# Agent attention and a maxout layer on one core: a new order of the whole program, with a rebuilt head, paired value products, five relu slots and split PSUM reads

## The chip, the cores and the metric

One core of a Trainium2 chip runs the whole program. The metric is the time of one execution in microseconds on the device; the kernel before took 438.34 us (median of three runs, 438.05 to 439.25).

## The reference

```
B, N, C, n_agents = 4, 12544, 128, 49;  d_ff = 768
sm(a, b)  = softmax(a @ b.T / sqrt(C))                 # over the last axis
agent_v   = sm(agents, k) @ v                          # 49 x 128 per batch
attn      = sm(q, agents) @ agent_v                    # 12544 x 128 per batch
x         = attn.reshape(50176, 128)
h         = max(max(x @ w1, x @ w2), x @ w3)           # 50176 x 768
out       = h @ w_out                                  # 50176 x 128
```

## The kernel before, in words

The attention output is never formed. For each batch the agents' values (49 x 128, normalised) are multiplied with weight differences into a matrix G: w3-w1 (768 columns at C31), w2-w1 (768 columns at C21), and w1 @ w_out (128 columns at C1O). A query's exponentials over the 49 agents, times G, then give the hidden layer's differences, and max(w1, w2, w3) becomes w1 + max(relu(w3-w1), w2-w1), of which the w1 part goes straight to the output (`li`). The division by the softmax's sum is done at the very end (`ov`).

**Key and value part.** Each batch has 98 tiles of 128 rows of k and v, taken in chunks (`FIRST` for batch 0, `LATER` for the others). For a chunk g of batch b: loads `kl`, `vl` on SP's DMA queue, casts to bf16 `kc`, `vc` (POOL; in batch 0 the values are cast by ACT), a transpose of the keys (batch 0: TensorE `kt` and DVE `ke`; later batches: a DMA transpose `kt` from the buffer KB to KT on SP's queue), scores `ks` (49 columns a tile), exponentials `kx` on ACT, products with the values `kv` on PE, and their addition `va` into VA on DVE. When a batch is done, `nr` normalises, and `gp`/`gv` make and copy G.

**Query part.** 49 steps s of eight tiles (1024 rows). Load `ql`, cast `qc` (POOL), transpose: `qd`, by DMA (QB to QT), for the steps in `TURNED`, else TensorE `qt` and DVE `qe`; scores `sc`, exponentials `ex` on ACT, sums `su`. Then for each of six 128-column blocks f of the hidden layer: `u` (PE, difference w3-w1, 128 x 1024 into a pair of PSUM banks), `a` (ACT relu into a slot of AS), `v` (PE, w2-w1, another pair of banks), `x` (DVE: maximum of v in PSUM and a, into R). Block FI = 4 does it without DVE: ACT relus into PSUM, PE adds, ACT relus into R. The output products `p` go either as full 128-row blocks or as pairs of 64-row blocks (`ROWS`, f or r); `ov` (DVE) scales into OS, `st` stores.

**What sets the order.** Nothing is decided at run time. `ORDER` is a written list of all operations with their slot numbers (`name/slots`); each engine issues its own in that order, and a wait is put wherever an operation needs another's result or slot. SP's one queue carries all loads, the DMA transposes and nearly all stores, and SP issues them in order: a transfer that must wait holds up those behind it. `SLOTS` gives the buffers: 8 PSUM banks (PS), 13 load buffers (LD), 10 output buffers (OS), 4 of KT, 4 of QT, 3 of AS, 13 of R. `SPLIT` marks the blocks whose u lies in two separate banks, which ACT reads as two relus of 512 columns.

**Head.** Before the first u, batch 0 must be through: 12.85 MB of keys and values at one DMA queue, then the weights, in halves. Meanwhile PE runs idle products of the identity (`wm`, `wn`).

Of the kernel before, what the change touches and what calls it, by code (L numbers as in the profile page):

```python
# [9 lines left out]
FP32 = mybir.dt.float32  # L10
BF16 = mybir.dt.bfloat16
# [6 lines left out]
DFF = NF * P  # L18
SCALE = 1.0 / math.sqrt(C)
C31, C21, C1O, WC = 0, DFF, 2 * DFF, 2 * DFF + C  # L20
CV, CT = KT * A, (KT - 1) * A
FI = 4
SPARE = 8
FIRST = [KT] * 10 + [4, 4]
LATER = [KT] * 10 + [8]
TURNED = (10, 13, 15, 18, 22, 24, 25, 28, 29, 30, 31, 32, 33, 34, 35, 36, 37, 38, 39, 40, 41, 42, 43, 44, 45, 46, 47, 48,)
ROWS = """
rrfrff rrrffr ffrfff ffrfrr rfffff rrrrrr ffffff ffffrr fffrff rfrrfr fffffr ffrfrf rrfrrr fffffr fffffr frffrf fffrrr rfffff
ffffff rrrfff ffffrf rrrfff rrffrr ffrrrr rrrrrr ffffff ffffff rrfffr ffrfrr rrrrrr ffffff ffffff fffffr rffrfr rrrrrr ffrffr
rfrrfr frrfff rrfrfr ffrffr rfffrr rrrrrr frffrf rfrfff rfrfff rrrfrr ffrfff rrrrrr rffrff  # L30
""".split()
# [11 lines left out]
ROW, FULL, COL = range(3)  # L43


SLOTS = {"PS": 8, "LD": 13, "QB": 3, "KB": 3, "VB": 4, "KT": 4, "QT": 4, "EQ": 4, "EK": 4, "AS": 3,
# [8 lines left out]
class Plan:  # L55
# [9 lines left out]
    def add(self, name, eng, fn, cost, mode=FULL, after=(), new=(), use=(), serve=0.0, dma=False, sides=None):  # L65
        self.index[name] = len(self.ops)
        for cls, t, *banks in new:
            self.tile(cls, t, *banks)
        self.ops.append(dict(name=name, eng=eng, fn=fn, pace=cost[0], lat=cost[1], mode=mode, after=list(after),
                             use=[x[1] for x in new] + list(use), serve=serve, dma=dma or eng == SP, sides=sides or {}))  # L70
# [89 lines left out]
    def lane(self, o, place, first):  # L160
        if not o["use"]:
            return "AG"
# [45 lines left out]
def graph(plan, em):  # L208
# [3 lines left out]
    add("id0", POOL, em.clear_ident, (0.3, 0.6))  # L212
    add("id", POOL, em.make_ident, (0.3, 0.6), after=["id0"])
    add("ones", DVE, em.make_ones, (1.0, 1.1), after=["id0"])
    add("agl", ACT, em.load_agents, (0.5, 5.0), dma=True)
    add("agc", DVE, em.cast_agents, (0.42, 0.52), after=["agl"])
    add("agt", PE, em.turn_agents, (0.2, 0.4), after=["agc", "id"], new=[("PS", "agt")])
    add("prep", DVE, em.place_agents, (0.4, 0.5), after=["agt", "ones"], use=["agt"])
    ch = chunks(0)
    for g, (t0, n) in enumerate(ch):  # L220
# [4 lines left out]
        add(f"kt0.{g}", PE, em.k_turn(g, n), mm(n, 128), after=[f"kc0.{g}", "prep"], new=[("PS", f"kT_ps0.{g}", 3)], use=[f"kb0.{g}"])  # L225
# [3 lines left out]
            new=[("EK", f"e0.{g}")], use=[f"s0.{g}"])  # L229
        add(f"to0.{g}", PE, em.totals(g, n), mm(1, n * 49), after=[f"kx0.{g}"], use=[f"e0.{g}", plan.tile("PS", "acc")])  # L230
# [3 lines left out]
        if m < n:  # L234
            add(f"vd0.{g}", DVE, em.cast("v", "vb", 0, t0, n, DVE, m, n), ((n - m) * 0.067 + 0.08, (n - m) * 0.067 + 0.2),
                after=[f"vl0.{g}"], use=[f"v0.{g}", f"vb0.{g}"])
        add(f"kv0.{g}", PE, em.first_values(g, n), mm(n, 49), after=[f"to0.{g}", f"vc0.{g}"] + ([f"vd0.{g}"] if m < n else []),
            use=[f"vb0.{g}", f"e0.{g}", "acc"])
    for g in range(SPARE):
        add(f"wm.{g}", PE, em.warm(f"warm.{g}"), (0.2225, 0.45), after=["id"], new=[("PS", f"warm.{g}")])  # L240
    for g in range(len(ch)):
        add(f"wn.{g}", PE, em.warm(f"warn.{g}", 2), (0.445, 0.67), after=["id", f"vl0.{g}"], new=[("PS", f"warn.{g}")])
    last = len(ch) - 1
    for w in ("w1", "w3", "w2"):
        add(f"l{w}a", SP, em.w_load(w, 0, DFF // 2), new=[("LD", w)], **dma(196))
        add(f"l{w}b", SP, em.w_load(w, DFF // 2, DFF), use=[w], **dma(196))
    add("lwo", SP, em.w_load("wo", 0, DFF), new=[("LD", "wo")], **dma(393))
    add("d31a", DVE, em.differences(C31, "w3", "w1", ((0, DFF // 2),)), (0.43, 0.55), after=["lw1a", "lw3a"], use=["w1", "w3"])
    add("d31b", DVE, em.differences(C31, "w3", "w1", ((DFF // 2, FI * P), (FI * P + P, DFF))), (0.42, 0.54), after=["lw1b", "lw3b"],
        use=["w1", "w3"])  # L250
    add("d32", DVE, em.differences(C31, "w3", "w2", ((FI * P, FI * P + P),)), (0.21, 0.33), after=["lw2b", "lw3b"], use=["w2", "w3"])
    add("d21a", DVE, em.differences(C21, "w2", "w1", ((0, DFF // 2),)), (0.43, 0.55), after=["lw2a", "lw1a"], use=["w1", "w2"])
    add("d21b", DVE, em.differences(C21, "w2", "w1", ((DFF // 2, DFF),)), (0.43, 0.55), after=["lw2b", "lw1b"], use=["w1", "w2"])
    add("cw1", ACT, em.cast_w1, (0.74, 0.87), after=["lw1a", "lw1b"], use=["w1"])
    add("tw1", PE, em.turn_w1, mm(NF, 128), after=["cw1", "prep"], new=[("PS", "tw1")])
    add("ew1", DVE, em.evacuate_w1, dve_half(DFF), after=["tw1"], use=["tw1"])
    add("cwo", POOL, em.cast_wo, (0.77, 0.85), after=["lwo"], use=["wo"])
    add("rs0", DVE, em.reduce_first, (0.5, 0.6), after=[f"to0.{g}" for g in range(last + 1)], new=[("KR", "kr0")], use=["acc"])
    add("rc0", DVE, em.recip_first, (0.35, 0.4), after=["rs0"], use=["kr0"])
    add("nr0", DVE, em.normalise_first, (0.13, 0.25), after=["rc0"] + [f"kv0.{g}" for g in range(last + 1)], new=[("G", "G0")],  # L260
        use=["kr0", "acc"])
    half = DFF // 2
    for name, c, d, eng in (("a", C31, ["d31a"], ACT), ("b", C31 + half, ["d31b", "d32"], DVE), ("c", C21, ["d21a"], ACT),
                            ("d", C21 + half, ["d21b"], DVE)):
        add(f"gp{name}", PE, em.product(0, c, c + half, f"gp{name}"), mm(1, half), mode=COL, after=["nr0"] + d, new=[("PS", f"gp{name}")])
        add(f"gv{name}", eng, em.product_out(0, c, c + half, c, f"gp{name}", eng), act(half) if eng == ACT else dve(half),
            after=[f"gp{name}"], use=[f"gp{name}", "G0"])
    add("pl", PE, em.prep_linear, mm(NF, 128), after=["ew1", "cwo"], new=[("PS", "pl")])
    add("el", ACT, em.evacuate_linear, (0.17, 0.31), after=["pl", "ones"], use=["pl"])
    add("gl", PE, em.product(0, C1O, WC, "gl"), mm(1, C), mode=COL, after=["nr0", "el"], new=[("PS", "gl")])  # L270
    add("gvl", ACT, em.product_out(0, C1O, WC, C1O, "gl", ACT), act(C), after=["gl"], use=["gl", "G0"])


    for b in range(1, B):
        ch = chunks(b)
        for g, (t0, n) in enumerate(ch):
# [11 lines left out]
            add(f"kv{r}", PE, em.values(b, g, n, m), mm(n, 49), after=[f"kx{r}", f"vc{r}"], use=[m, f"vb{r}", f"e{r}"])  # L288
            add(f"va{r}", DVE, em.add_values(b, g, m), (0.13, 0.25), after=[f"kv{r}"] + ([f"va{b}.{g - 1}"] if g else []),
                use=[m, plan.tile("VA", f"va{b}")])  # L290
# [7 lines left out]
        add(f"to{b}", PE, em.total(b, g, n, m), (n * 0.0253 + 0.1, n * 0.0253 + 0.335), after=[f"fo{b}", f"kv{r}"],  # L298
            use=[m, f"es{b}", f"e{r}"])
        held = [f"gp{x}" for x in "abcd"] + ["gl"] if b == 2 else [f"gp{x}{b - 2}" for x in "abcdl"] if b > 2 else []  # L300
        add(f"kr{b}", DVE, em.reciprocal_of(b, m), (0.25, 0.3), after=[f"to{b}"], new=[("KR", f"kr{b}")], use=[m])
        add(f"nr{b}", DVE, em.normalise(b, m), (0.25, 0.32), after=[f"kr{b}", f"va{r}"] + held, new=[("G", f"G{b}")],
            use=[f"kr{b}", f"va{b}"])
        for name, c0, c1, eng in (("a", C31, C31 + half, ACT), ("b", C31 + half, C21, DVE), ("c", C21, C21 + half, ACT),
                                  ("d", C21 + half, C1O, DVE), ("l", C1O, WC, ACT)):
            w = c1 - c0
            add(f"gp{name}{b}", PE, em.product(b, c0, c1, f"gp{name}{b}"), mm(1, w), mode=COL,
                after=[f"nr{b}", "el", "d31a", "d31b", "d32", "d21a", "d21b"], new=[("PS", f"gp{name}{b}")])
            add(f"gv{name}{b}", eng, em.product_out(b, c0, c1, c0, f"gp{name}{b}", eng), act(w) if eng == ACT else dve(w),
                after=[f"gp{name}{b}"], use=[f"gp{name}{b}", f"G{b}"])  # L310
# [744 lines left out]
```

## Time and profile before

| what | value |
|---|---|
| median of three runs | 438.34 us |
| span of the profiled execution | 436.6 us; the page gives no other time of it |
| granted TensorE clock, mean | 0.996 |
| PE / DVE / ACT / POOL busy | 411.9 / 386.6 / 393.9 / 170.0 us |
| first u on PE | 41.41 us |
| moved by DMA | 122.37 MB, mean 280 GB/s |
| DMA transposes | 33 of keys, 28 of queries |

A busy share is the time in which an instruction of the engine is under way. On ACT and DVE the records of neighbours overlap, so what an instruction costs in a row of them is the distance from its start to the next one's. The tile names are the buffer classes above, with `ps` for the PSUM banks. All instructions carry the line of the helper that records them, so that the rows are told apart by tiles and shapes.

### The profile page before, as it was taken

How to read it: one execution, taken by the hardware profiler on the slowest of the kernel's cores; microseconds unless marked ns; L12 is line 12 of the kernel's file. 1: busy time of each engine (PE TensorE's matmuls, PEld its weight loads, DVE VectorE, ACT ScalarE, POOL GpSimd, SP SyncE). 2: the span in 40 equal slices, each digit the busy share in tenths (PEclk: the TensorE clock that was granted, in tenths of full speed). 3: DMA queues.
4: the chain of work that ended last, by engine and by line, in shares of the span. 5: the costliest groups of instructions: out<-in, count | busy, mean ns of one | idle time of the engine just before them, and what ended most of it. 6: DMA issues, size and time to landing. Idle time of an engine off the chain costs nothing.

```text
span 436.6 us, 14853 instructions
## 1 busy us (share of the span) xinstructions
PE 411.9 (94%) x6488; PEld 256.9 (59%) x6488; DVE 386.6 (89%) x470; ACT 393.9 (90%) x486; POOL 170.0 (39%) x177
## 2 busy tenths in 40 slices
PE   1788999999999999999999999999999999999994
PEld 1464565666666566656656655656656555655574
DVE  1435999999999999999998999899999999999994
ACT  1278999999999999999999899999999999999993
POOL 3541565556655535165525445342531111000000
PEclk9989999999999999999999999999999999999999
DMA  8999999999999999999999999996999994266313
GB/s 310 411 410 383 311 334 372 289 281 343 269 318 342 279 371 298 266 339 285 294 345 261 407 247 278 276 326 143 276 363 290 284 306 98 74 208 208 119 71 125
DMA packets 98107, 122.37 MB, mean 280 GB/s; under 512 B 71479, under 2 KB 74235, under 8 KB 98043
## 3 DMA queue, kind: packets, MB, share of 16 engines
q1 hardware_dynamic: 97552, 121.07, 95.2%
q8 instruction: 51, 0.84, 0.8%
q10 hardware_dynamic: 491, 0.36, 0.3%
q14 instruction: 13, 0.11, 0.1%
HBM read 78.74 MB, written 25.69 MB: 239 GB/s over the span
## 4 chain that ended last, share of the span: by engine, by line
PE 69%; ACT 16%; DVE 7%; DMA 4%; issue 2%; POOL 1%; SPq 0%; POOLq 0%
PE ps L388 69%; ACT AS L388 9%; DVE R L388 6%; DMA LD<-in_k_dram 4%; ACT R L388 2%; ACT ps L388 2%; POOL KB L388 1%; DVE OS L388 1%; ACT EQ L388 1%; ACT VB L388 1%; ACT G L388 1%; ACT EK L388 1%; ACT OS L388 0%; SPq L388 0%; DVE QT L388 0%
## 5 line engine op out<-in xcount | busy, mean ns | idle before, releaser
L388 DVE TENSOR_TENSOR R<-ps,AS 128x1024 bf16<-128x1024 f32 x245 | 293.5, 1219 | 15.1 <-PE ps L388 10.7
L388 ACT ACTIVATE AS<-ps 128x1024 bf16<-128x1024 f32 (+1 forms) x259 | 245.8, 987 | 10.0 <-PE ps L388 7.2
L388 PE MATMUL ps<-EQ,G 49*128 49x512 bf16 (+1 forms) x1248 | 203.3, 370 | 3.5 <-ACT AS L388 0.7
L388 PE MATMUL ps<-wo_bf,R 64*128 64x128 bf16 (+1 forms) x3368 | 194.0, 218 | 1.1 <-issue 0.8
L388 PEld LDWEIGHTS ps<-wo_bf,R 64*128 64x128 bf16 (+1 forms) x3368 | 139.5, 95 | 59.4 <-issue 31.3
L388 PEld LDWEIGHTS ps<-EQ,G 49*128 49x128 bf16 x1248 | 56.4, 93 | 63.8 <-DVE R L388 18.3
L388 POOL CAST QB<-LD 128x1024 bf16<-128x1024 f32 x49 | 50.5, 1040 | 94.6 <-DMA QT<-QB 49.8
L388 POOL CAST KB<-LD 128x1152 bf16<-128x1152 f32 (+2 forms) x45 | 49.8, 1115 | 52.1 <-DMA LD<-in_k_dram 41.8
L388 DVE TENSOR_TENSOR OS<-ps,RC 128x512 f32<-128x512 f32 x96 | 65.4, 682 | 2.6 <-PE ps L388 2.2
L388 POOL CAST VB<-LD 128x1152 bf16<-128x1152 f32 (+1 forms) x33 | 37.4, 1136 | 40.7 <-DMA LD<-in_v_dram 36.5
L388 ACT ACTIVATE ps<-ps 128x1024 f32<-128x1024 f32 x49 | 49.9, 1018 | 2.8 <-PE ps L388 2.2
L388 ACT ACTIVATE R<-ps 128x1024 bf16<-128x1024 f32 x49 | 50.3, 1027 | 1.9 <-PE ps L388 1.6
L388 ACT ACTIVATE EK<-ps 128x441 bf16<-128x441 f32 (+2 forms) x45 | 23.4, 535 | 18.8 <-PE ps L388 18.4
L388 POOL TENSOR_TENSOR EA<-EA,EK 128x441 f32<-128x441 f32 x27 | 27.6, 1022 | 25.4 <-ACT EK L388 25.1
L388 ACT ACTIVATE EQ<-ps 128x512 bf16<-128x512 f32 x49 | 29.9, 610 | 1.0 <-PE ps L388 0.5
L388 DVE COPY KT<-ps 128x1152 bf16<-128x1152 bf16 (+1 forms) x12 | 8.2, 701 | 14.0 <-PE ps L388 14.0
L388 PE MATMUL ps<-QT,agT 128*64 128x512 bf16 (+1 forms) x104 | 19.9, 388 | 0.2
L388 PE MATMUL ps<-G,EQ 49*128 49x128 bf16 x392 | 19.1, 217 | 0.0
L388 PE MATMUL ps<-EK,VB 128*128 128x49 bf16 x392 | 17.4, 186 | 1.6 <-ACT VB L388 1.6
L388 PEld LDWEIGHTS ps<-EK,VB 128*128 128x128 bf16 x392 | 13.9, 97 | 8.1 <-ACT EK L388 4.2
L388 PE MATMUL ps<-agT,KT 128*128 128x49 bf16 x392 | 17.4, 186 | 0.4 <-DVE KT L388 0.4
L388 PEld LDWEIGHTS ps<-agT,KT 128*128 128x128 bf16 x392 | 14.4, 98 | 4.7 <-issue 2.1
(59 smaller groups left out, 177.6 us busy)
## 6 DMA issues: line engine op xcount, KB each, us to landing
LD<-in_q_dram SPq DMA_DIRECT2D x48, 512.0 KB, 7.7
out_dram<-OS SPq DMA_DIRECT2D x48, 512.0 KB, 6.2
LD<-in_k_dram SPq DMA_DIRECT2D x40, 576.0 KB, 7.6
LD<-in_v_dram SPq DMA_DIRECT2D x40, 576.0 KB, 8.4
LD<-in_k_dram SPq DMA_DIRECT2D x3, 512.0 KB, 5.3
LD<-in_v_dram SPq DMA_DIRECT2D x3, 512.0 KB, 6.7
LD<-in_moe_w_dram SPq DMA_DIRECT2D x6, 192.0 KB, 10.6
KT<-KB SPq DMA_TRANSPOSE x33, 7.3
```

What stands on the lines that cost most here:

```text
L388: i = call(*args, **named)
```

## The change

- **Head.** Batch 0 comes in twelve chunks of 8 tiles and one of 2 (`FIRST`), all keys ahead of nearly all values. Ten of the value chunks are loaded into the output buffers OS, exponentials of batch 0 go into R slots, and scratch tiles of their own (agents, w1) go into R slots too. The casts of the values are dealt out by `VCAST` (seven to POOL, five to ACT, one to DVE). The weights come in three pieces (128, 256, 384 columns, `CUTS`) instead of two, and the first G is made in matching pieces. The cast of w1 goes to POOL and behind the first step's products, and w_out is loaded behind that.
- **Values in pairs.** For batches 1 to 3 the value products of two chunks go into one bank of their own, followed by one addition: 18 `va` instead of 33. They no longer share the bank of the scores.
- **Splits.** `SPLIT` now knows u (two relus), v (two maxima of 512 columns) and b (both): 85 blocks of 245 have split relus (14 before), 72 split maxima (none before). An operation d, for a DVE relu in block FI, is written and not used.
- **Slots.** AS has five slots instead of three.
- **Linear part.** G's last part is stored twice, each for 64 rows with zeros in the other half (`gz`), so that `li` could also run as full blocks; `LINEAR` uses the old way for all 49.
- **Query turns.** Steps 20, 21 and 23 are turned by DMA too: 31 `qd` instead of 28.
- **64-row blocks.** 116 of 294 output blocks are pairs of 64 rows, 127 before.
- **Order and slots** of the whole program are new.

```
-FIRST = [KT] * 10 + [4, 4]
+CUTS = {"a": (0, P), "b": (P, 3 * P), "c": (3 * P, DFF)}
+FIRST = [GT] * 12 + [2]
-TURNED = (10, 13, 15, 18, 22, 24, 25, 28, ...
+TURNED = (10, 13, 15, 18, 20, 21, 22, 23, 24, 25, 28, ...
 SPLIT = """
-...... u..... .u.... ...... ...... ...... ...... ...... ...... ...... .u.u.. uu.... ...
+vvv..b vbvv.v .u.u.. b..u.u v.uu.v bbbb.u ...u.u .uub.u v.vb.b .uub.. .u.u.u vvuu.v ...
...
+LINEAR = "bbbbbbbbbbbbbbbbbbbbbbbbbbbbbbbbbbbbbbbbbbbbbbbbb"
+VCAST = "pppaappapaapd"
+CASTW = "p"
+OUTS = ("aaaaadd", "addda", "addda", "adada")
-SLOTS = {"PS": 8, "LD": 13, "QB": 3, ... "EK": 4, "AS": 3,
+SLOTS = {"PS": 8, "LD": 13, "QB": 3, ... "EK": 4, "AS": 5,
...
-        add(f"vl0.{g}", SP, em.kv_load("v", 0, t0, n), new=[("LD", f"v0.{g}")], **dma(n * 65.536))
+        add(f"vl0.{g}", SP, em.kv_load("v", 0, t0, n), new=[("OS" if g < 10 else "LD", f"v0.{g}")], **dma(n * 65.536))
...
-        m = n if n == KT else 2
-        add(f"vc0.{g}", ACT, em.cast("v", "vb", 0, t0, n, ACT, 0, m), act(m * 128), after=[f"vl0.{g}"], new=[("VB", f"vb0.{g}")],
+        eng = ENGINES[VCAST[g]]
+        add(f"vc0.{g}", eng, em.cast("v", "vb", 0, t0, n, eng, 0, n), act(n * 128), after=[f"vl0.{g}"], new=[("VB", f"vb0.{g}")],
             use=[f"v0.{g}"])
...
-            add(f"kv{r}", PE, em.values(b, g, n, m), mm(n, 49), after=[f"kx{r}", f"vc{r}"], use=[m, f"vb{r}", f"e{r}"])
-            add(f"va{r}", DVE, em.add_values(b, g, m), (0.13, 0.25), after=[f"kv{r}"] + ([f"va{b}.{g - 1}"] if g else []),
+            if g % 2 or g == len(ch) - 1:
+                two = [(x, ch[x][1]) for x in range(g // 2 * 2, g + 1)]
+                y, h = f"{b}.{g // 2}", f"y{b}.{g // 2}"
+                add(f"kv{y}", PE, em.values(b, two, h), mm(sum(x[1] for x in two), 49), after=[f"{z}{b}.{x}" for x, _ in two for z in ("kx", "vc")],
+                    new=[("PS", h)], use=[f"{z}{b}.{x}" for x, _ in two for z in ("vb", "e")])
+                add(f"va{y}", DVE, em.add_values(b, g // 2, h), (0.13, 0.25), after=[f"kv{y}"] + ([f"va{b}.{g // 2 - 1}"] if g > 1 else []),
...
+                if SPLIT[s][f] in "vb":
+                    vs = [f"{v}.{h}" for h in range(2)]
+                    add(v, PE, em.hidden(vs, s, f, C21, True), pe, mode=ROW, after=[f"ex.{s}"] + needs(1), new=[("PS", x) for x in vs],
+                        use=[e] + gs)
+                    for h in range(2):
+                        add(f"x.{s}.{f}.{h}", DVE, em.max_second(vs[h], s, f, h), (0.6, 0.72), after=[v, f"{a}.{h if SPLIT[s][f] == 'b' else 0}"],
+                            use=[vs[h], a, r])
```

Three places of the order, before and after. In these rows a name is a buffer (its number is the compiler's), `OUT<-IN`, then the shape; `LD` are load buffers, `KB`/`QB` cast keys and queries, `KT`/`QT` their transposes.

First, SP's queue in the second half of batch 3. The row `KT_104<-KB_96 128x9x128` before (row 197 of SP) is the key transpose of that batch's chunk 9, the last of 9 tiles:

```order
L388 DMA_TRANSPOSE QT_105<-QB_93 128x8x128
L388 DMA LD_86<-in_q_dram 128x1024
L388 DMA_TRANSPOSE KT_104<-KB_95 128x9x128
L388 DMA out_dram<-OS_139 128x1024
L388 DMA_TRANSPOSE QT_108<-QB_92 128x8x128
L388 DMA LD_82<-in_v_dram 128x1152
L388 DMA_TRANSPOSE KT_104<-KB_96 128x9x128
L388 DMA LD_86<-in_k_dram 128x1024
```

After, the same transpose is `KT_99<-KB_90 128x9x128`, row 212 of SP:

```order
L416 DMA_TRANSPOSE QT_103<-QB_87 128x8x128
L416 DMA LD_84<-in_q_dram 128x1024
L416 DMA LD_77<-in_v_dram 128x1152
L416 DMA_TRANSPOSE QT_104<-QB_88 128x8x128
L416 DMA LD_78<-in_k_dram 128x1152
L416 DMA out_dram<-OS_144 128x1024
L416 DMA LD_86<-in_q_dram 128x1024
L416 DMA LD_79<-in_v_dram 128x1152
L416 DMA_TRANSPOSE KT_99<-KB_90 128x9x128
L416 DMA_TRANSPOSE KT_100<-KB_92 128x8x128
```

It stood behind 196 transfers and now stands behind 209: the key load of 512 KB that followed it is now far ahead, and so are three more query loads and four more query transposes; the other five are loads of the head in more pieces.

Second, PE around the scores of that chunk (`ps<-agT,KT`), before:

```order
L388 MATMUL ps<-EQ_109,G_149 128x512 x4
L388 MATMUL ps<-wo_bf,R_132 128x128 x4
L388 MATMUL ps<-wo_bf,R_120 128x128 x4
L388 MATMUL ps<-agT,KT_104 128x49 x9
L388 MATMUL ps<-EQ_109,G_149 128x512 x6
```

and after:

```order
L416 MATMUL ps<-EQ_105,G_147 128x512 x4
L416 MATMUL ps<-wo_bf,R_120 128x128 x4
L416 MATMUL ps<-wo_bf,R_124 128x128 x4
L416 MATMUL ps<-agT,KT_99 128x49 x9
L416 MATMUL ps<-EQ_105,G_147 128x512 x6
```

The scores have kept their place among the hidden products (rows 914 and 916 of PE); what has moved is the transpose on SP's queue.

Third, ACT at the end of the head, before (`VB<-LD` casts values, `G` is the first G, `AS` the first relus):

```order
L388 ACTIVATE VB_99<-LD_90 128x1152
L388 ACTIVATE VB_100<-LD_80 128x1152
L388 ACTIVATE EQ_112<-ps 128x512
L388 ACTIVATE VB_97<-LD_82 128x1152
L388 ACTIVATE w_bf<-LD_85 128x768
L388 ACTIVATE G_147<-ps 128x384 x2
L388 ACTIVATE AS_117<-ps 128x1024
```

and after:

```order
L416 ACTIVATE VB_96<-OS_140 128x1024
L416 ACTIVATE VB_94<-OS_143 128x1024
L416 ACTIVATE G_145<-ps 128x256
L416 ACTIVATE G_145<-ps 128x128
L416 ACTIVATE G_145<-ps 128x256
L416 ACTIVATE G_145<-ps 128x128
L416 ACTIVATE AS_113<-ps 128x1024
```

The last value casts have gone to POOL, the cast of w1 too, the query exponentials stand earlier, and four smaller copies of G stand where two larger ones stood.

More of the change, by code (lines that the diff above doesn't have):

```diff
@@ L63, in tile, with add @@
         return name
-    def add(self, name, eng, fn, cost, mode=FULL, after=(), new=(), use=(), serve=0.0, dma=False, sides=None):
+    def add(self, name, eng, fn, cost, mode=FULL, after=(), new=(), use=(), serve=0.0, dma=False, sides=None, lane=None):
         self.index[name] = len(self.ops)
@@ L252, in graph @@
[L252 to L256, printed above, removed]
+    for x, (c0, c1) in CUTS.items():
+        cuts = ((c0, FI * P), (FI * P + P, c1)) if x == "c" else ((c0, c1),)
+        add(f"d31{x}", DVE, em.differences(C31, "w3", "w1", cuts), dve(c1 - c0), after=[f"lw1{x}", f"lw3{x}"], use=["w1", "w3"])
+        add(f"d21{x}", DVE, em.differences(C21, "w2", "w1", ((c0, c1),)), dve(c1 - c0), after=[f"lw1{x}", f"lw2{x}"], use=["w1", "w2"])
@@ new lines, in graph @@
+                add(f"a.{s}.{f}.0", ACT, em.relu(u, u, None), (0.917, 1.076), after=[u], use=[u])
+                add(v, PE, em.hidden([u], s, f, C21, False), pe, mode=ROW, after=[f"a.{s}.{f}.0"] + needs(1), use=[u, e] + gs)
+                if SPLIT[s][f] == "d":
+                    add(f"x.{s}.{f}.0", DVE, em.relu(r, u, None, DVE), (1.14, 1.28), after=[v], use=[u, r])
+                else:
+                    add(f"x.{s}.{f}.0", ACT, em.relu(r, u, None), (0.917, 1.076), after=[v], use=[u, r])
@@ L352, in graph @@
                 else:
-                    add(u, PE, em.hidden([u], s, f, C31, True), pe, mode=ROW, after=[f"ex.{s}"] + needs("a", "b"), new=[("PS", u, 3)], use=[e] + gs)
-                    add(a, ACT, em.relu(a, u, None), (0.917, 1.076), after=[u], use=[u, a])
-                add(v, PE, em.hidden([v], s, f, C21, True), pe, mode=ROW, after=[f"ex.{s}"] + needs("c", "d"), new=[("PS", v, 3)], use=[e] + gs)
-                add(f"x.{s}.{f}", DVE, em.max_second(v, s, f), (1.14, 1.28), after=[v] + ([f"{a}.{h}" for h in range(2)] if two else [a]),
-                    use=[v, a, r])
@@ L358, in graph @@
-        lin = ["gvl" if p[0] == 0 else f"gvl{p[0]}" for p in parts]
+                    add(u, PE, em.hidden([u], s, f, C31, True), pe, mode=ROW, after=[f"ex.{s}"] + needs(0), new=[("PS", u, 3)], use=[e] + gs)
+                    add(f"{a}.0", ACT, em.relu(a, u, None), (0.917, 1.076), after=[u], use=[u, a])
+                if SPLIT[s][f] in "vb":
[5 more added lines that the diff above has]
+                            use=[vs[h], a, r])
+                else:
+                    add(v, PE, em.hidden([v], s, f, C21, True), pe, mode=ROW, after=[f"ex.{s}"] + needs(1), new=[("PS", v, 3)], use=[e] + gs)
+                    add(f"x.{s}.{f}.0", DVE, em.max_second(v, s, f, None), (1.14, 1.28), after=[v] + [f"{a}.{h}" for h in range(1 + (SPLIT[s][f] == "u"))],
+                        use=[v, a, r])
```

651 lines of the change are left out of this document (348 added, 303 removed).

## The prediction

> **What bounds the kernel now.** I read the page first (span, busy shares, the row of the DMA engines), then the busy time by stage, then the waits, then the transfers by kind, and last single stretches of the timeline.
>
> ```profile
> span 436.6 us, 14853 instructions
> PE 411.9 (94%) x6488; PEld 256.9 (59%) x6488; DVE 386.6 (89%) x470; ACT 393.9 (90%) x486; POOL 170.0 (39%) x177
> ...
> DMA  8999999999999999999999999996999994266313
> ```
>
> Three engines stand near 90%, so none of them alone is the answer. The last line is the one that I follow: the DMA engines are full in every slice up to the 34th of 40, and idle behind it. By stage, from the busy time in stretches (the last two numbers of a row are the DMA share and GB/s):
>
> ```profile
> 10.00:20.00 10.00, 7.44 (x87) 5.08 (x86) 4.11 (x7) 2.22 (x6) 5.33 (x6) 1.00 1.03 412
> ...
> 50.00:100.00 50.00, 49.49 (x821) 31.48 (x820) 47.88 (x58) 47.24 (x59) 28.47 (x28) 1.00 1.11 320
> ...
> 300.00:350.00 50.00, 49.44 (x752) 29.57 (x750) 48.27 (x56) 48.78 (x60) 15.86 (x19) 1.00 1.07 283
> 350.00:400.00 50.00, 49.56 (x768) 29.63 (x766) 48.52 (x53) 48.93 (x57) 5.20 (x5) 1.00 0.57 173
> 400.00:425.00 25.00, 24.76 (x442) 15.73 (x442) 24.25 (x26) 23.82 (x28) 0.00 (x0) 1.00 0.33 116
> ```
>
> Between 10 and 20 us nothing but loads is under way, many deep, and the share reads 1.03: that is what a full queue looks like here. From 50 to 350 us it reads 1.07 to 1.11. From 350 us on it falls to 0.57 and 0.33: there the transfers are done and ACT and DVE set the pace, with DVE idle 1.73 + 1.48 + 0.75 = 4.0 us between 300 and 425 us. The waits say the same from the other end:
>
> ```profile
> POOL KB L388 <- DMA LD<-in_k_dram: 41.8, 17, 5.9
> POOL VB L388 <- DMA LD<-in_v_dram: 36.5, 18, 4.6
> ...
> PEld ps L388 <- DVE R L388: 18.6, 74, 0.6
> ...
> PEld ps L388 <- ACT AS L388: 16.0, 61, 0.6
> ```
>
> POOL starts a key or value cast when the load lands, 35 times. PE itself never stands long for a transfer; it waits 0.1 to 0.6 us at a time for a PSUM bank that DVE or ACT still reads. So up to about 330 us two limits run side by side, the bank turnover and the transfer queue, and I have to price the queue.
>
> **The price of a transfer.** Transfers by kind, of the 250 us in which the share is full, and of the loads alone in the head:
>
> ```profile
> q1 hardware_dynamic: 66112, 75.88, 109.2%
> ...
> LD<-in_v_dram SPq DMA_DIRECT2D x29, 576.0 KB, 7.4
> LD<-in_k_dram SPq DMA_DIRECT2D x28, 576.0 KB, 7.6
> LD<-in_q_dram SPq DMA_DIRECT2D x31, 512.0 KB, 8.1
> out_dram<-OS SPq DMA_DIRECT2D x22, 512.0 KB, 6.5
> LD<-in_k_dram SPq DMA_DIRECT2D x2, 512.0 KB, 6.0
> LD<-in_v_dram SPq DMA_DIRECT2D x2, 512.0 KB, 6.9
> KT<-KB SPq DMA_TRANSPOSE x30, 7.5
> QT<-QB SPq DMA_TRANSPOSE x13, 7.3
> ```
> ```profile
> DMA packets 1772, 6.51 MB, mean 407 GB/s; under 512 B 196, under 2 KB 320, under 8 KB 1770
> ```
>
> At 407 GB/s a tile of 128 rows (65.5 KB) takes 0.161 us, a 512 KB transfer 1.29 us. The loads and stores of the 250 us are 57 x 9 + 57 x 8 = 969 tiles, 156 us. If the queue was full, the remaining 94 us went to the 43 transposes, 372 tiles: 0.253 us a tile, 2.0 us for a query tile's transpose of 8. That is the upper end. The lower end is their bytes alone at 407 GB/s: 0.64 us for 256 KB; then 64 of the 250 us would have been idle, which a share of 109% does not allow. The full share is the nearer row, so I take 2.0 us, and treat what the queue lay idle as time that comes back.
>
> **The change, part by part.** *Transfers.* Batch 3's key transpose of chunk 9 is SP's row 197 before and row 212 after, and PE's scores on it stand at nearly the same place (rows 914 and 916). Counted along the queue, 8 more transfers lie ahead of it in the new order: three query loads, one key load of 512 KB (which followed it before) and four query transposes (three because query tiles 20, 21 and 23 are now turned by DMA, one because a later tile's is issued sooner). The other five places are loads cut finer, with the same bytes. Work ahead of it: 4 x 1.29 = 5.2 us, and 4 x 2.0 = 8.1 us, together 13.3 us. What it had to spare:
>
> ```profile
> 292.76 0.49 SPq L388 DMA_DIRECT2D LD<-in_v_dram  x1
> 300.52 1.45 SPq L388 DMA_TRANSPOSE KT<-KB  x1
> ```
> ```profile
> DMA to landing us min/median/max: 3.2/3.8/4.5
> ```
> ```profile
> 298.91 1.14 POOL L388 CAST VB<-LD 128x1152 bf16<-128x1152 f32 x1 [4.62 <-DMA LD<-in_v_dram]
> ...
> 314.48 1.04 POOL L388 CAST VB<-LD 128x1024 bf16<-128x1024 f32 x1 [2.10 <-DMA LD<-in_v_dram]
> ```
> ```profile
> 306.78 0.39 PE L388 MATMUL ps<-agT,KT 128*128 128x49 bf16 x9
> ```
>
> It was issued at 300.52 and landed at the earliest 3.2 us later, 303.7; PE used it at 306.78: 3.1 us to spare. SP issued nothing between 293.3 and 300.5 (it stood before this transpose), and the value load that it had issued last was cast from 298.9, as soon as it had landed, so the queue lay empty for some 3 us. In the new order SP has a backlog there, and those 3 us come back. So PE meets this tile late by 13.3 - 3.1 = 10.2 us at the upper end, and by 7.2 us with the 3 us back; each further microsecond that the queue was idle in the 306 us before takes one off, down to no lateness at all (the first rival). I take **+6 us**, since one gap is seen and the share leaves little room for others. What is late next is everything behind those scores in PE's order (the hidden products of step 32 and 33), and through them ACT and DVE, which run dry; the queries' transposes behind it on SP are late by as much.
>
> The Trainium skill's page "DMA: Bandwidth & Descriptors", section "Latency and other measured facts", gives a DMA transpose an effective 261 GB/s: 1.0 us for a query tile and 1.1 for a key tile, estimates from that page. By it the 43 transposes would fill 47 of the 94 us, the queue would have idled for the other 47 and taken the new transfers without lateness, and the time would be that of the first rival. The share of 109% speaks against it.
>
> *Head.* The last value cast, and what follows it:
>
> ```profile
> 38.47 1.16 ACT L388 ACTIVATE VB<-LD 128x1152 bf16<-128x1152 f32 x1
> 39.66 0.84 ACT L388 ACTIVATE w_bf<-LD 128x768 bf16<-128x768 f32 x1
> ...
> 41.90 3.87 ACT L388 ACTIVATE AS<-ps 128x1024 bf16<-128x1024 f32 x4
> ```
>
> The same bytes must land first, so the landing does not move. The cast goes to POOL, where 1024 columns take 1.04 us (the POOL row at 314.48) against 1.16 here, and no longer stands behind ACT's other casts; the first copies are 256 wide instead of 384. That is -0.7 us (0 to -1.5), and it is spent where PE next waits for a transfer: nothing of it reaches the end.
>
> *Splits, pairs, turns.* Start to start, back to back:
>
> ```profile
> 199.04 1.23 DVE L388 TENSOR_TENSOR R<-ps,AS 128x1024 bf16<-128x1024 f32 x1
> 200.18 0.68 DVE L388 COPY QT<-ps 128x1024 bf16<-128x1024 bf16 x1
> 200.78 0.45 DVE L388 TENSOR_TENSOR VA<-ps,VA 128x49 f32<-128x49 f32 x2
> ...
> 202.61 0.68 DVE L388 TENSOR_TENSOR OS<-ps,RC 128x512 f32<-128x512 f32 x1
> 203.21 1.22 DVE L388 TENSOR_TENSOR R<-ps,AS 128x1024 bf16<-128x1024 f32 x1
> ```
> ```profile
> 202.90 1.02 ACT L388 ACTIVATE AS<-ps 128x1024 bf16<-128x1024 f32 x1
> 203.81 0.59 ACT L388 ACTIVATE EQ<-ps 128x512 bf16<-128x512 f32 x1
> 204.30 1.02 ACT L388 ACTIVATE R<-ps 128x1024 bf16<-128x1024 f32 x1
> ```
>
> DVE's maximum holds it 1.14 us, a PSUM read of half the width 0.60; a split costs 0.06. ACT: 0.91 against 0.49, 0.07. The table goes from 14 to 85 split relus and from none to 72 split maxima: ACT +5.0 us, DVE +4.3. DVE loses 15 value additions of at most 0.22 (-3.3) and three query copies of 0.60 (-1.8): -0.8 in sum. PE loses three query turns. It gets 22 more full-array output blocks, and before such blocks it paid:
>
> ```profile
> L388 PEld LDWEIGHTS ps<-wo_bf,R 128*128 128x128 bf16 x1336 | 75.6, 97 | 34.2 <-issue 28.8 <-DVE OS L388 2.7 <-DVE VA L388 0.7
> ```
>
> 28.8 us over 334 groups of four is 0.09 us each, +1.9 us. None of this moves the end before 306.8 us, where the transfers cover it. What the splits buy is that the first bank of a pair comes free about half a read sooner (0.91 - 0.49 or 1.14 - 0.60), and the pairs of value products no longer hold a scores bank. After the late tile that can win at most DVE's idle time of 4.0 us; I take half, -2.0 (0 to -4.0), and +0.5 for the splits that lie there. The fifth relu slot I cost at nothing: no row of the waits has ACT waiting for a relu slot. POOL's seven value casts in the head (7.3 us) lie beside a POOL that is half idle (5.33 of 10 us); if that cover fails, the last cast is late by one cast, 1.0 us.
>
> Sum: 436.6 + 6.0 - 2.0 + 0.5 = 441.1 us span. The runs' median, 438.34, is 1.74 above the profiled span (the page gives no other time of that execution), so **442.8 us**.
>
> **Rivals.** *Faster: the queue has room after all.* Then 8 more transfers cost nothing, and the head and the banks show. DVE is idle 2.1 us between 50 and 100 us; five such stretches and the later 4.0 make 14.6 us, ACT's extra 5.0 us come off, and I take half of the rest, -4.8. 436.6 - 0.7 - 4.8 + 1.7 = 432.8 us. For it: PE has no long wait for a transfer now, and SP did leave the queue empty at 299. Against it: the share. It decides if the queue idled for about 10 of the 306 us before that tile, which is all that it takes: a mean transpose of 1.95 us instead of 94 / 43 = 2.19. The rule of 261 GB/s lies far on that side of the point.
>
> *Slower for another reason: the engines.* Transfers hidden, no idle time won, ACT's 5.0 us added and the head's 0.7 taken off: 442.6 us. Against it: ACT's waits are for PE's banks, which come free sooner.
>
> *No change:* late by 2 to 3 us at chunk 9, and as much won back behind it: 438 us.
>
> **How the numbers follow.** Late transfers 0.52, engines 0.08, no change 0.13, room in the queue 0.27. Runs of this kernel spread by 0.3%, about 1.3 us, which I take as the bound of "same". So slower 0.60, same 0.13, faster 0.27. The likeliest case by itself reaches from 438 (3 us late, 4.0 us won back) to 449 (10.2 us late, nothing won back: 436.6 + 10.2 + 0.5 + 1.7). Downward the range takes in the slower half of the faster case: 434 to 449.
>
> **What would show it.** In the new profile PE's scores of batch 3, chunk 9, start between 309 and 316 us, after an idle time put down to a transpose; the DMA share stays at 1.07 or more past 340 us; POOL's waits for loads grow; PE has waits of over 1 us that it lacks now. If instead those scores start before 306 us and the share falls below 1.0 earlier, the queue had room and I am wrong on the price of a transpose. The first relu should start near 41.2 us.

## The result and the profile after

The changed kernel takes 443.31 us (median of 14 runs, 439.56 to 446.28); the kernel before, run beside it, 438.67 us (14 runs, 437.89 to 440.07). The ratio is 1.0095, with a 95% interval of 1.0071 to 1.0119. The medians are 4.6 us apart; the ratio, which leaves out one of the 14 executions (446.28 us) because it ran in the chip's slower state, gives 4.2 us. The profiled execution took 444.69 us, with a span of 442.3, so 2.39 us lie outside the span, against 1.74 before; over all runs it is 2.35 against 1.78.

The head of the new page, with the row of the granted TensorE clock:

```profile
span 442.3 us, 14868 instructions
PE 418.7 (95%) x6396; PEld 262.0 (59%) x6396; DVE 388.5 (88%) x529; ACT 389.7 (88%) x553; POOL 178.8 (40%) x190
...
PEclk9999999999999799999989999999999999999998
DMA  8999999999999999999999999999998919346216
```

The clock row before:

```profile
PEclk9989999999999999999999999999999999999999
```

PE is busy 6.8 us longer than before with fewer instructions, and the clock row has a 7 and an 8 where it had 9s. By stage (after the length come PE, its weight loads, DVE, ACT and POOL, busy us with the number of instructions; then the clock, the DMA share and GB/s), first after:

```profile
100.00:150.00 50.00, 47.55 (x687) 29.56 (x686) 46.68 (x64) 46.73 (x72) 26.94 (x29) 0.99 1.09 320
150.00:200.00 50.00, 49.80 (x736) 30.85 (x735) 46.51 (x64) 45.84 (x65) 26.14 (x26) 0.94 1.12 291
200.00:250.00 50.00, 48.32 (x759) 30.04 (x759) 44.05 (x63) 46.42 (x71) 22.46 (x25) 0.97 1.08 309
...
300.00:350.00 50.00, 49.34 (x719) 29.51 (x716) 47.86 (x62) 48.61 (x67) 18.04 (x20) 1.00 1.01 282
350.00:400.00 50.00, 49.65 (x760) 29.54 (x758) 48.95 (x56) 49.03 (x61) 4.26 (x5) 1.00 0.48 137
400.00:425.00 25.00, 24.78 (x387) 14.80 (x388) 24.91 (x30) 24.70 (x33) 0.00 (x0) 1.00 0.40 128
```

and three of these stages before:

```profile
100.00:150.00 50.00, 49.77 (x752) 30.30 (x750) 47.85 (x61) 47.77 (x63) 30.77 (x33) 1.00 1.10 316
150.00:200.00 50.00, 49.82 (x796) 31.51 (x797) 47.85 (x57) 48.36 (x59) 21.97 (x21) 1.00 1.12 302
200.00:250.00 50.00, 49.76 (x821) 31.10 (x819) 46.38 (x58) 47.08 (x62) 25.14 (x27) 1.00 1.10 324
```

The loss lies between 100 and 250 us, not past 306. Matching the first hidden product of each step by the order gives the lateness against before: +0.6 us at step 12 (140.5 us against 139.9), +5.2 at step 13, +3.8 at step 20, +6.5 at step 22 (234.9 against 228.4), and +6.3 still at step 32. The first jump, on POOL and then on PE:

```profile
130.82 1.15 POOL L416 CAST VB<-LD 128x1152 bf16<-128x1152 f32 x1
138.71 1.15 POOL L416 CAST KB<-LD 128x1152 bf16<-128x1152 f32 x1 [6.73 <-DMA LD<-in_k_dram]
145.31 1.15 POOL L416 CAST KB<-LD 128x1152 bf16<-128x1152 f32 x1 [5.45 <-DMA LD<-in_k_dram]
146.40 1.04 POOL L416 CAST QB<-LD 128x1024 bf16<-128x1024 f32 x1
147.39 1.15 POOL L416 CAST KB<-LD 128x1152 bf16<-128x1152 f32 x1
148.48 1.15 POOL L416 CAST VB<-LD 128x1152 bf16<-128x1152 f32 x1
```
```profile
149.69 0.93 PE L416 MATMUL ps<-EK,VB 128*128 128x49 bf16 x18 [2.06 <-POOL VB L416]
```

POOL takes its casts in order and stands 6.73 us for the load of batch 2's key chunk 4 and then 5.45 us for that of chunk 3. Behind both stands the value cast of chunk 1 (148.48), though SP had issued the load of its tile at 91.15 us. PE wants that cast for the pair of chunks 0 and 1 and waits 2.06 us. In the new order ten more transfers lie ahead of chunk 3's key load (three value, two key and two query loads, a store, a key and a query transpose). SP issues it as the second of two at 134.6 us, where it stood at 119.9 before. That these ten transfers make it late is read from the order and these times; no run put the load back. SP's rows of after, then of before:

```profile
91.15 0.33 SPq L416 DMA_DIRECT2D LD<-in_v_dram  x1
...
134.11 0.94 SPq L416 DMA_DIRECT2D LD<-in_k_dram  x2
```
```profile
119.87 0.77 SPq L388 DMA_DIRECT2D LD<-in_k_dram  x1
```

The second jump is the same with chunk 10's value cast, behind a key load that POOL waits 1.73 us for:

```profile
222.99 1.14 POOL L416 CAST KB<-LD 128x1152 bf16<-128x1152 f32 x1 [1.73 <-DMA LD<-in_k_dram]
...
224.40 1.04 POOL L416 CAST VB<-LD 128x1024 bf16<-128x1024 f32 x1
```
```profile
225.58 0.37 PE L416 MATMUL ps<-EK,VB 128*128 128x49 bf16 x8 [1.15 <-ACT R L416]
```

The profile puts this PE wait down to an ACT instruction that ended at about the same time; the product reads POOL's cast, which ends at 225.43. After both of these waits PE runs at half its clock:

```profile
145.00:150.00 5.00, 2.94 (x45) 1.77 (x42) 3.31 (x3) 3.58 (x7) 4.69 (x5) 0.93 1.01 410
150.00:155.00 5.00, 5.00 (x51) 2.82 (x50) 3.94 (x6) 3.02 (x4) 2.21 (x3) 0.50 1.25 182
155.00:160.00 5.00, 5.00 (x102) 3.56 (x98) 3.27 (x4) 4.05 (x8) 0.00 (x0) 0.89 1.11 160
225.00:230.00 5.00, 4.28 (x44) 2.21 (x46) 3.13 (x7) 3.52 (x5) 3.02 (x5) 0.78 1.24 306
230.00:235.00 5.00, 4.82 (x90) 3.15 (x84) 3.81 (x5) 4.32 (x6) 0.00 (x0) 0.88 1.07 228
```

From 150 to 155 us PE is fully busy and does half the matmuls of the next five. The clock that is missing adds up to (0.07 + 0.50 + 0.11) x 5 = 3.4 us at the first place and (0.22 + 0.12) x 5 = 1.7 at the second. A busy PE at 0.50 looks like no idle time at all; only the clock column shows it.

### The profile page after: what moved, and what is told of

It is laid out like the page before. It is cut to its first block, busy times and chain, and to the rows that moved or that the text cites. A ratio compares the mean times of both kernels' runs of the same rounds, so it can differ in the third digit from the quotient of the medians.

```text
span 442.3 us, 14868 instructions
## 1 busy us (share of the span) xinstructions
PE 418.7 (95%) x6396; PEld 262.0 (59%) x6396; DVE 388.5 (88%) x529; ACT 389.7 (88%) x553; POOL 178.8 (40%) x190
## 4 chain that ended last, share of the span: by engine, by line
PE 55%; DMA 11%; ACT 11%; DVE 8%; issue 7%; POOL 6%; SPq 1%; POOLq 0%; DVEq 0%
PE ps L416 55%; ACT AS L416 6%; DVE R L416 6%; DMA LD<-in_k_dram 5%; DMA LD<-in_v_dram 3%; DMA KT<-KB 3%; POOL VB L416 2%; ACT R L416 2%; POOL KB L416 2%; ACT ps L416 1%; POOL QB L416 1%; DVE OS L416 1%; SPq L416 1%; POOL EA L416 1%; ACT EQ L416 1%
## 5 line engine op out<-in xcount | busy, mean ns | idle before, releaser
L416 DVE TENSOR_TENSOR R<-ps,AS 128x512 bf16<-128x512 f32 (+1 forms) x317 | 297.5, 974 | 15.6 <-PE ps L416 10.9
L416 ACT ACTIVATE AS<-ps 128x1024 bf16<-128x1024 f32 (+1 forms) x330 | 250.4, 816 | 12.0 <-PE ps L416 9.6
L416 PE MATMUL ps<-wo_bf,R 64*128 64x128 bf16 (+1 forms) x3286 | 197.1, 219 | 0.6 <-ACT EK L416 0.3
L416 PEld LDWEIGHTS ps<-wo_bf,R 64*128 64x128 bf16 (+1 forms) x3286 | 142.0, 96 | 63.1 <-issue 34.2
L416 ACT ACTIVATE R<-ps 128x1024 bf16<-128x1024 f32 (+1 forms) x58 | 54.7, 946 | 9.2 <-PE ps L416 9.0
L416 POOL CAST VB<-LD 128x1152 bf16<-128x1152 f32 (+1 forms) x34 | 38.4, 1138 | 23.0 <-DMA LD<-in_v_dram 22.3
L416 ACT ACTIVATE EK<-ps 128x441 bf16<-128x441 f32 (+2 forms) x37 | 19.7, 537 | 18.7 <-PE ps L416 18.6
L416 DVE COPY KT<-ps 128x1024 bf16<-128x1024 bf16 (+1 forms) x13 | 8.3, 658 | 10.8 <-PE ps L416 10.8
L416 PEld LDWEIGHTS ps<-G,EQ 49*128 49x128 bf16 x392 | 13.8, 96 | 4.9 <-PE ps L416 0.9
L416 PE MATMUL ps<-EK,VB 128*128 128x49 bf16 x320 | 12.0, 187 | 3.7 <-POOL VB L416 2.6
```

Of the source, the lines that this page charges most:

```text
L416: i = call(*args, **named)
```

## The experiments

Theory A: two waits behind POOL's order and the half clock behind them are the loss. Theory B: the transfers are late, and these places only show it. Theory C: the splits load the engines. The kernel before took 438.81 us beside the first eight kernels (two groups of four), 438.89 beside the next three and 438.41 beside the last.

**The two casts ahead.** Rows of the order table moved:

```diff
- vc2.3 kc2.4 kc2.3 qc.15 kc2.2 vc2.1 qc.16
+ vc2.3 vc2.1 kc2.4 kc2.3 qc.15 kc2.2 qc.16
- vc3.3 ea2.9 fo2.0 kc3.2 fo2.1 vc2.10 fo2.2
+ vc3.3 vc2.10 ea2.9 fo2.0 kc3.2 fo2.1 fo2.2
```

> The changed kernel with two value casts moved ahead in POOL's order: chunk 1 of batch 2 ahead of the two key casts that wait for their loads, chunk 10 of batch 2 ahead of the key cast of batch 3's chunk 2. Theory A (two PE waits behind POOL's order, and the halved TensorE clock after each, are the whole loss): PE's waits of 2.2 us near 148 and 1.2 us near 225 are gone, the granted clock reads 1.00 from 50 to 425 us, and the time falls by 5 to 8 us, to 435.5 to 438.5. Theory B (the full transfer queue sets the pace, these waits are only where it shows): PE waits at the next late transfer instead, the time stays within 1.5 us of 443.3. Theory C (the added splits load the engines): the waits go and the time stays at 442 to 443.

443.99 us (ratio 1.0132, 1.0105 to 1.0159). Theory A fell. Both waits are gone, and the kernel runs ahead of before until step 18 (194.4 us against 195.5); then PE meets other transfers. Busy time by stretch, and the PE timeline of the profile:

```profile
150.00:155.00 5.00, 5.00 (x100) 3.11 (x94) 4.57 (x6) 4.79 (x8) 0.00 (x0) 1.00 1.13 150
195.00:200.00 5.00, 2.73 (x55) 2.09 (x54) 2.88 (x4) 2.80 (x6) 2.54 (x3) 1.00 1.26 244
205.00:210.00 5.00, 2.27 (x24) 1.07 (x22) 3.07 (x5) 3.66 (x4) 2.24 (x2) 1.00 0.84 235
210.00:215.00 5.00, 4.15 (x62) 3.09 (x64) 1.46 (x2) 1.60 (x2) 0.00 (x0) 0.70 1.08 265
```
```profile
210.85 0.41 PE L416 MATMUL ps<-QT,agT 128*64 128x512 bf16 x2 [3.57 <-DMA QT<-QB]
```

The tile that PE waits for here is the transpose of query tile 21, one of the three newly turned by DMA. Ahead of it PE waits 1.10 and 1.16 us for the transposes of key chunks 8 and 7.

**PE kept busy through the two waits.**

```diff
+FILL = {'2.0': 9, '2.5': 5}
+add(f"wf{y}", PE, em.warm(h, FILL[y]), ..., new=[("PS", h)])   # ahead of kv{y} in the order
```

> The changed kernel with 9 and 5 extra 512-column matmuls on PE (0.22 us each, their results overwritten by the products behind them), put just ahead of the two pairs of value products that wait for POOL, so that PE is busy while it would have waited. Theory A, with the clock as a loss of its own: the lateness of the waits stays, the granted clock stays at 1.00 near 150 and 228 us, and the time falls by 3 to 5 us, to 438 to 440.5. If the halved clock costs nothing because DVE and ACT set the pace there, or if it follows from something else than PE's idleness: 443 to 444. Theory B: 443 to 444.

442.92 us (1.0102, 1.0069 to 1.0135). In its profile the clock stays at 1.00, and step 13 starts at 156.9 us instead of 160.9, though 1.6 of these 4.0 us it had already at step 12, ahead of the first wait. PE then waits 1.15 us for query tile 21's transpose, and the median moves by 0.4 us only. Being late by less there means meeting the transfers earlier.

**One cast behind, in the kernel before.**

```diff
- vc2.0 kc2.3 qc.15 (kv2.0 on PE) vc2.1
+ kc2.3 qc.15 vc2.1 vc2.0 (kv2.0 on PE)
```

> The kernel before with one value cast (chunk 0 of batch 2) moved behind the next value cast in POOL's order, which waits for its load until 137.6 us: PE, which wants the product at 136.7, should wait some 3 us (until 139.9). Theory A: the granted clock falls to 0.50 for 3 to 7 us behind the wait, and the time grows by more than the wait, by 4 to 6.5 us, to 442.5 to 445. If a wait costs only itself: +2 to +3, 440.7 to 441.7. If the transfer queue gets ahead during the wait and gives it back: +0 to +1, 438.7 to 439.7.

444.51 us (1.0135, 1.0116 to 1.0155), +5.7. The wait was longer than planned, 4.6 us on PE, since the load landed later. POOL's row, PE's row and the stretches:

```profile
138.80 2.24 POOL L388 CAST VB<-LD 128x1152 bf16<-128x1152 f32 x2 [4.55 <-DMA LD<-in_v_dram]
```
```profile
141.09 0.55 PE L388 MATMUL ps<-EK,VB 128*128 128x49 bf16 x9 [4.57 <-POOL VB L388]
```
```profile
135.00:140.00 5.00, 1.53 (x16) 0.62 (x12) 2.08 (x4) 2.61 (x4) 1.20 (x2) 1.00 1.14 280
140.00:145.00 5.00, 3.91 (x29) 1.88 (x31) 2.15 (x4) 1.89 (x3) 5.00 (x5) 0.55 1.08 400
145.00:150.00 5.00, 5.00 (x72) 2.94 (x68) 3.22 (x4) 3.62 (x5) 1.78 (x3) 0.77 1.14 271
```

**The same with PE kept busy.**

```diff
+add("wf", PE, em.fill(m, 27), mm(27, 384), use=[m])   # ahead of kv2.0 in the order
```

> The kernel of cast_behind (444.5) with 27 matmuls of 384 columns (0.16 us each, 4.4 us, into a part of the bank that nothing reads afterwards) put ahead of the product that waits 4.7 us for its cast, so that PE is busy through the wait. If PE's idleness is what halves its clock, and the halved clock is part of the loss: the granted clock stays at 1.00 from 135 to 150 us and the time falls by 1.5 to 3 us, to 441.5 to 443. If the halved clock costs nothing because DVE and ACT have to catch up anyway: 444 to 445.

441.16 us (1.0052, 1.0033 to 1.0071), a little below what I expected. The late product alone costs 2.3 us; the half clock costs the other 3.35 us (each with some 1.2 us of uncertainty). The clock missing in the rows above is (0.45 + 0.23) x 5 = 3.4 us, so here, by the medians, all of it reached the end.

**Light stores, both kernels.**

```diff
-queue.dma_start(out[r, :]...("(p j) c -> p j c", j=n), os[:, cut, :])
+queue.dma_start(out[r, :]...("(p j) c -> p j c", j=n)[:, :1, :], os[:, cut.start:cut.start + 1, :])
```

> The changed kernel with every store cut to one of its eight 64-column blocks (64 KB instead of 512 KB; the other rows of the output are not written), so that the queue has some 1.1 us less to do for each of the stores. Theory B and theory A agree that the loads then land early enough: no PE wait over 1 us between 50 and 425 us, clock at 1.00, and the gain of the banks shows: 431 to 436. Theory C (engines, splits): the time stays at 440 to 443.

> The kernel before with every store cut to one of its eight 64-column blocks (the other rows of the output are not written), as in light_after, which took 436.9. If the kernel before was held by the queue too, as I argued from its full share: 434 to 436.5, and the change is worth nothing even with room in the queue. If it was held by banks and engines: 438 to 439, and the rest of the change is worth 1.5 to 2 us once the queue has room.

After: 436.86 us (0.9958, 0.9938 to 0.9977), just above my 431 to 436. Before: 437.16 (0.9966, 0.9953 to 0.9979), between my two values. As expected, the profile of light_after has the clock at 1.00 throughout, and PE's longest wait between 50 and 425 us is 0.93 us. The lighter queue gives the changed kernel 443.31 - 436.86 = 6.45 us and the kernel before 438.81 - 437.16 = 1.65. The difference, 4.8 us, is the whole loss: theory B, with the waits of theory A as the way in which late transfers reach PE. All the rest of the change is worth 0.3 us, within the uncertainty. The stretch from 50 to 330 us, of before, light_before and light_after in this order:

```profile
50.00:330.00 280.00, 277.83 (x4394) 172.99 (x4394) 265.71 (x322) 268.18 (x337) 140.47 (x143) 1.00 1.09 303
```
```profile
50.00:330.00 280.00, 277.42 (x4384) 172.62 (x4384) 266.12 (x321) 267.98 (x337) 141.04 (x145) 1.00 0.99 264
```
```profile
50.00:330.00 280.00, 276.33 (x4302) 172.49 (x4300) 266.02 (x366) 270.01 (x394) 143.37 (x146) 1.00 1.01 275
```

The DMA share hardly falls when seven eighths of the stores' bytes are gone, 1.09 to 0.99: here a share near 1 did not say that there was no room.

**The splits joined again**, 86 of 157, in light_after.

```diff
-vvv..b vbvv.v .u.u.. b..u.u ...
+ (only the halves whose two banks are no neighbours stay split)
```

> light_after with 86 of the 157 split reads joined again (those whose two PSUM banks are neighbours: 53 relus and 33 maxima, each one instruction of 1024 columns instead of two of 512), the stores cut as there. If the splits win bank time, as I argued: 1 to 3 us slower than light_after's 436.9, 438 to 440. If their extra 0.06 to 0.07 us each sits on the path: 1 to 4 us faster, 433 to 436. If neither: 436 to 437.5.

446.12 us (1.0170, 1.0152 to 1.0188), 9.3 us slower than light_after: theory C fell, and by three times what I thought they could win. PE's waits for relus between 50 and 330 us, light_fewer_splits first, then light_after:

```profile
PEld ps L416 <- ACT AS L416: 15.7, 45, 0.9
```
```profile
PEld ps L416 <- ACT AS L416: 10.0, 38, 0.5
```

**Turns given back to PE**, three and ten, in the kernel of casts_ahead.

```diff
-TURNED = (10, 13, 15, 18, 20, 21, 22, 23, 24, 25, 28, ...
+TURNED = (10, 13, 15, 18, 22, 24, 25, 28, ...      # turns_back
+TURNED = (28, ...                                  # turns_more
```

> The kernel of casts_ahead with query tiles 20, 21 and 23 turned by PE and copied by DVE again, as before the change (three transposes fewer in the transfer queue, three turns and copies more on PE and DVE). Theory B at my price of 2.0 us a transpose: the queue has 6 us less to do ahead of step 21, the waits for the transposes of key chunks 7 and 8 (1.3 us each) and of query tile 21 (3.7 us), and the halved clock behind them, are gone or nearly so, and the time falls by 4 to 7 us from 444.0, to 437 to 440. At half that price (1.0 us) part of the wait stays: 440.5 to 442. If the queue isn't what PE waited for: 444 to 446, since the engines get 0.5 and 0.6 us more for each.

> The kernel of casts_ahead with query tiles 10, 13, 15, 18 and 20 to 25 turned by PE (ten transposes fewer in the queue). Theory B: the queue falls behind nowhere, no PE wait of over 1 us for a transfer, and the banks' gain shows less the engines' 10 x 0.5 us: 435 to 439. If the engines' load decides once the queue has room: 440 to 442.

442.15 us (1.0080, 1.0058 to 1.0101) and 454.35 (1.0346, 1.0322 to 1.0370), the first just above what I expected at half my price, the second far above both of my ranges. With three, the waits for those transposes are gone but only 1.8 of the expected 4 to 7 us come back, and with ten the time grows by 10 us. I had put the PE turns wherever the order left a bank free, and PE waits for banks at nearly each of them (the waits from 105 to 270 us, in turns_more and then in casts_ahead):

```profile
PEld ps L416 <- DVE R L416: 11.7, 29, 1.6
DVE QT L416 <- PE ps L416: 8.9, 10, 3.2
```
```profile
PEld ps L416 <- DVE R L416: 6.4, 24, 0.5
```

These two mix the queue's relief with the price of a bank. The next two relieve the queue alone.

**The three transposes cut short, or copied plainly**, in the kernel of casts_ahead.

```diff
+if dst == "qT." and r in (20, 21, 23):
+    dma_start(qT[:, :1, :], qb[:, :1, :])      # short_turns
+    dma_start(qT[:, :n, :], qb[:, :n, :])      # copied_turns
```

> The kernel of casts_ahead (444.0) with the three new query transposes of tiles 20, 21 and 23 cut to a plain copy of one of their eight blocks (32 KB; those three tiles' scores are computed from wrong data), so that the queue is relieved of them and no engine gets more to do. Theory B: the PE wait of 3.7 us for query tile 21 and the halved clock behind it are gone, 437.5 to 440.5; the rest to light_after's 436.9 is what the other transfers still cost. If the three have no part in it: 443 to 445.

> The same with those three transposes replaced by plain copies of all their bytes (256 KB each; wrong data for those tiles' scores too). If a transpose costs the queue 2.0 us and its bytes alone 0.64 us, as I took: within 1.5 us of short_turns, 438 to 441. If a transpose costs what its bytes cost: no better than casts_ahead, 443 to 445.

439.63 us (1.0006, 0.9987 to 1.0026) and 439.57 (1.0031, 1.0005 to 1.0056), both 4.4 us better than casts_ahead by the medians (5.5 and 4.4 by the ratios, each with some 1.5 us of uncertainty). So the three transposes cost some 4.4 us there, 1.5 each as a mean, and it is the transposing that costs, not the 256 KB.

**One part alone: the three transposes in the kernel before.**

```diff
-TURNED = (10, 13, 15, 18, 22, 24, 25, 28, ...
+TURNED = (10, 13, 15, 18, 20, 21, 22, 23, 24, 25, 28, ...
- qt.20 qe.20 ... qt.21 qe.21 ... qt.23 qe.23
+ vl2.10 qd.20 qd.22 st.17 qd.21 ... qd.24 qd.23
```

> The kernel before with one part of the change alone: query tiles 20, 21 and 23 turned by DMA instead of PE and DVE; their transposes stand in SP's order directly behind the last transfer that SP had issued before their casts were ready, all else keeps its order. If the three transposes are the loss (theory B, 4.4 us for the three by short_turns): 441.5 to 444, with PE waits or late casts behind step 20. If the kernel before had room for them where its own queue ran empty: 438 to 439.5, and the loss of the change needs its other moved transfers too. If PE and DVE gain more than the queue loses: 436.5 to 438.

442.59 us (1.0101, 1.0082 to 1.0119), +4.2, although PE and DVE have three turns and copies less to do. Nearly all of it arises at one place: the profile is 0.2 us ahead of before at step 21 and 4.4 us behind at step 22. Tile 23's transpose is issued at 220.8 us, behind tile 24's, and lands at 224.8. At 222.7 and 224.8 us PE waits for POOL and for tile 23's transpose, and the clock follows:

```profile
224.80 0.64 PE L388 MATMUL ps<-QT,agT 128*64 128x512 bf16 x2 [1.14 <-DMA QT<-QB]
```
```profile
225.00:230.00 5.00, 5.00 (x52) 2.77 (x52) 2.42 (x4) 2.98 (x4) 0.00 (x0) 0.50 1.00 389
```

The clock that is missing around it is 3.4 us. So this one part gives nearly the loss of the whole change, but through one late tile and the half clock behind it: a third of the 4.2 us is a mean, not the price of one transpose. In the full change the first lateness comes earlier, most likely from the ten transfers moved ahead of a key load; that hides the three transposes, which appear as soon as it is taken away (casts_ahead). With both gone the loss is gone (short_turns, within 0.3% of before). A kernel with the transposes cut short and the two casts left in place was not run, so it is not shown that both must go.

## Why the prediction was right in size and wrong in place

The forecast was 442.8 us and the kernel takes 443.3. That the two are half a microsecond apart is luck: the transfers cost 1.2 us less than I put down, and the rest of the change won 1.2 us less (0.3 where I had 1.5 in sum: -2.0 and +0.5). The mechanism, late transfers on SP's queue that PE ends up waiting for, was right; the place was not.

**Transfers, +6 us.** Right in kind, and 4.8 us by the pair of light kernels. What I had wrong is the place. I followed one path, a transpose that PE reads directly, batch 3's chunk 9. Its scores did start at 313.3 us, inside my 309 to 316, but not because of the tile: PE was already 6.3 us late, and the transpose had landed with 4 us to spare.

```profile
313.26 0.39 PE L416 MATMUL ps<-agT,KT 128*128 128x49 bf16 x9
```

The path that I left out is load, POOL's order, PE: a load that is late holds every cast behind it, of tiles that landed long ago too. A pair of value products needs the later of two casts, which makes such a hold reach PE. The list of moved transfers would have shown it at the key load of chunk 3 in the same way. I also read the DMA row of before as full in every slice up to the 34th; it has a 6 in the 28th, about 295 to 305 us, and a 4 in the 34th.

**The price of a transpose, 2.0 us.** Measured 1.4 to 1.5 of time as a mean (4.2 and 4.4 us for three, half clock included); what one costs depends on whether its tile is late for PE. The Trainium skill, page "DMA: Bandwidth & Descriptors", section "Latency and other measured facts", gives 1.0 us by its 261 GB/s, an estimate from that page; the runs lie midway between that and my 2.0. My way to 2.0 was wrong: it read the share of 109% as a full queue, and light_before shows 0.99 with far less to move. A candidate in its place is SP itself. In casts_ahead:

```profile
181.21 0.46 SPq L416 DMA_DIRECT2D out_dram<-OS  x1
181.72 10.19 SPq L416 DMA_TRANSPOSE KT<-KB  x1
191.95 0.58 SPq L416 DMA_DIRECT2D out_dram<-OS  x1
```

A load takes SP some 0.45 us to issue; this transpose, with eight transfers issued and not yet landed ahead of it, held SP for 10.19 us, and nothing further was requested meanwhile. The three query transposes hold SP for 10.3 us in that kernel, and for 1.7 us as plain copies (copied_turns). That fits a price of SP's standing and not of the bytes. The sum over the kernel does not: from 50 to 330 us the transposes hold SP for 149.6 us before (49 of them), 144.3 after and 149.1 in casts_ahead (51 each), and 150.7 in turns_alone, which is 4.2 us slower than before. Which part of a transpose is its price stays open.

**The half clock.** It is in no step of mine. It cost 3.35 us behind one wait (cast_behind against behind_filled), by the medians more than the late product itself. I priced a wait at its length. In the changed kernel its share of the 4.6 us was not isolated, since filled_waits lost its gain to the next transfers.

**Head, -0.7 us.** Not seen. In this profile the first relu starts later than before (41.90), as ACT waits for the product ahead of it. Over the nine profiles with the new head it starts at 41.4 us in the mean (40.7 to 42.1), over the five with the old one at 41.5 (41.1 to 41.9), so there is no gain beyond the spread. After:

```profile
41.25 1.00 ACT L416 ACTIVATE G<-ps 128x256 bf16<-128x256 f32 x4 [2.73 <-PE ps L416]
42.12 1.96 ACT L416 ACTIVATE AS<-ps 128x1024 bf16<-128x1024 f32 x2
```

**Splits and banks, -2.0 and +0.5.** DVE is idle 3.3 us from 300 to 425 us instead of 4.0 (the sum over the three stages), so 0.7 rather than 2.0 was won there. Over the whole kernel, the light pair give 434.4 against 435.4 us of span by the medians of their executions. That the new order cannot do without its splits (9.3 us) says nothing for the change: the order before does as well with 14 split relus.

**The time outside the span** grew by 0.57 us; I carried over the old 1.74. Its cause stays open.

**The rivals.** Room in the queue: with room made for it the change gives 436.9 us, not 432.8; my 4.8 us of bank gain was too much. Engines, 442.6: light_after has all splits and takes 436.9. **The signs.** PE waits of over 1 us that it lacked: two, as said. POOL's waits for key loads grew (41.8 to 45.0 us), those for value loads fell (36.5 to 22.3). The share past 340 us does not stay at 1.07: it is 0.48 from 350 to 400 us, where it was 0.57 before, and 0.40 from 400 to 425, where it was 0.33.

## What to carry to other kernels

Where one engine takes its work in order, count what a moved transfer holds back on that engine, not only who reads the transfer; a cast whose data landed long ago can be the late one. Look for half clock behind each PE wait, in the clock column where PE reads "busy": here waits of 1 us and more were followed by 0, 1.7 or 3.4 us of missing clock. A late place that is repaired shows the next one, so the relief of a shared resource is measured best with that resource lightened in both kernels.

## What the runs showed that I had not expected

- A PE wait of 2.06 us was followed by 3.4 us of missing clock, one of 1.15 us by 1.7 us, one of 4.6 us by 3.4 us. Others were followed by none: 1.10 and 1.16 us in casts_ahead, 1.15 in filled_waits, 1.16 and 1.40 in turns_more. So the wait's length alone does not decide it, and what does is not shown. In these traces the half clock comes in stretches of 3.4 or 6.8 us. The Trainium skill, page "TensorE: Matmul & The Clock Gate", section "Part 1: The HAM clock gate", says that the array falls to half its clock after an idle window of about 3.4 us; the half agrees with the 0.50 here, but waits shorter than such a window were enough.
- Three plain copies of 256 KB between SBUF tiles took as long as three short transfers (439.57 us against 439.63) where three transposes of the same bytes took 4.4 us more.
- A transpose can hold SP for 10.19 us, against some 0.45 us for a load. Its least was 1.24 us.
